# A first stage's order written anew: local attention and a PReLU feed-forward on one Trainium2 core

## The chip, the cores and the metric

The kernel runs on one core of one Trainium2 chip. The metric is the device time of one execution in microseconds (us), the median of several runs. Lower is better. The reference runs in fp32, and the kernel keeps fp32 accuracy by splitting operands into a high and a low fp32r part.

## The reference

Attention is local: each sequence of 576 positions is cut into chunks of 64, and a chunk attends to itself alone. The result, 4608 tokens of 512 numbers, goes through two dense layers with a PReLU between them.

```python
scores = scale * np.matmul(q_c, k_c.transpose(0, 1, 2, 4, 3))     # 8 x 8 x 9 chunks of 64 x 64
scores = scores - np.max(scores, axis=-1, keepdims=True)
attn = np.exp(scores)
attn = attn / (np.sum(attn, axis=-1, keepdims=True) + 1e-09)
out = np.matmul(attn, v_c)
x = np.ascontiguousarray(out.transpose(0, 2, 1, 3)).reshape(B * S, H * D)   # 4608 x 512
h = x @ w_in                                                      # 512 -> 2048
g = np.maximum(h, 0.0) + alpha * np.minimum(h, 0.0)
return (g @ w_out).astype(np.float32)                             # 2048 -> 512
```

## The kernel before

**Tiles.** Tokens come in sub-blocks of 128 (two chunks, all eight heads); four sub-blocks make a block of 512 tokens, nine blocks in all. The first three blocks use plain matmuls, the other six go in pairs with fewer products; that later part isn't touched. The weights of both layers come as 16 chunks each (`wi0` to `wi15` of w_in, `wo0` to `wo15` of w_out). Each is loaded as raw 64-bit words and turned into a high and a low part by seven steps on ScalarE (ACT) and VectorE (DVE) (`piece`, L180).

**The first stage** prepares the eight sub-blocks of blocks 0 and 1 and the first nine chunks of each side, and starts the dense layers. Its order is written out by hand in `START` (L28): a list of tokens that a loop (L931) turns into instructions one after the other, so each engine runs its share in just that order. After the list a scheduler places the rest. The tokens are:

- `q`, `k`, `v` with a number: a load of that sub-block's operand (sub-blocks 0 and 1 one by one, then two at a time). `wi3`, `wo3`: the load of a raw chunk.
- `W5`: five filler matmuls 128x128 of zeros on TensorE (PE), whose result nobody reads (L898).
- `S3`: the scores of sub-block 3 on PE, 16 matmuls 64x64 (L261). `m3`: their maxima on DVE (L298). `z3`, `e3`, `a3`, `r3`, `n3`: the rest of the softmax. In the usual way `z` scales the maxima, `e` is eight exponentials on ACT, one per head, each with its own bias and with a summing read-out (L313), `a` adds 1e-9 on GpSimd (POOL). For the sub-blocks in `SUBTRACTED`, `z` subtracts the maxima on DVE (L302), `e` is one exponential over all heads (L304), and `a` sums on DVE (L307). `n` multiplies by the reciprocals.
- `T3`: four transposes of the probabilities on PE (L349); `p3`: ACT copies them out (L356). `V3`: times the values on PE, 16 matmuls 64x64 (L367); `x3`, `l3`: high part by ACT (L373), low part by DVE (L375).
- `h02`: first layer of block 0, chunk 2, 12 matmuls 128x512 on PE (L422); `R`, `G`, `gh`, `gl`: the PReLU and the split (L407, L410, L436, L439). `o02`: second layer, 12 matmuls (L458). `K`: a result tile is stored (L492, L495).
- `wi3b`, `k`, `h`, `u`, `v`, `i`, `j`: the seven steps of chunk `wi3` (L194 to L209); `b` and `i` run on ACT, the others on DVE. A chunk named in `ALONE` has all steps on DVE.

`BANKS` says which pair of PSUM banks each S, T and V takes (`banks_of`, L243): 0, 1 and 2 are the pairs `ps_a`, `ps_oa`, `ps_ob`. Before, a transpose takes a whole pair and uses one bank of it. The fillers and the first layer rotate through the two buffers of `ps_h`. `HALVES` names the scratch tile of each chunk's split.

Of the kernel before, what the change touches and what calls it, by code (L numbers as in the profile page):

```python
# [10 lines left out]
F32 = mybir.dt.float32  # L11
# [8 lines left out]
def bits(pattern):  # L20
# [5 lines left out]


START = """  # L28
W8 q0 k0 k1 q1 q2 S0 W1 k2 m0 S1 W5 wi1 z0 m1 e0 wi0 z1 a0 e1 r0 S2 k4 n0 S3 m2 q4 wi1b z2 T0 W6 m3
e2 a1 z3 wi1k v0 wi0b r1 wi1h n1 wi2 p0 wi0k T1 a2 e3 wi0h r2 S4 W3 v2 wi0u n2 m4 q6 p1 V0 a3 z4  # L30
wi0v e4 T2 W4 k6 r3 wi0i wi1u wi0j wo4 wi1v x0 V1 n3 p2 wo0 l0 x1 V2 wi2b a4 l1 T3 x2 wo1 wi2k S5 p3
l2 wi1i V3 m5 v6 S6 r4 x3 z5 n4 e5 wi4 l3 h00 m6 v4 wi2h z6 wi1j e6 wi2u S7 wi3 a5 wi2v h01 m7 wo2
r5 R00 z7 n5 wo0b G00 wi5 wi2i T5 e7 wo0k wi2j h02 wi7 a6 wo0h r6 wo0u wo5 n6 p5 wo0v gh00 T6 wo1b
a7 T4 wo3 gl00 wo0i V5 r7 wo1k p6 wo0j x5 V6 n7 p4 l5 x6 T7 wo1h V4 l6 p7 wo1u x4 o00 R01 wo1v wo2b
G01 wo1i l4 gh01 wo1j R02 V7 gl01 o01 x7 wo2k G02 wi4b wi3b wo2h wo2u gh02 l7 h10 wo2v gl02 wo2i
wi3k wo2j wi4k wo4b o02 wi3h wi4h R10 wo4k wi4u K0 wi3u K1 G10 h11 wi4v gh10 wi3v wi4i gl10 K2 wi3i
wo4h wi4j K3 o10 wo4u wo5b wi3j R11 wo4v wi5b G11 wo4i wo6 h12 wo5k gh11 wo4j wi6 gl11 wo3b wo5h
wo3k wo5u wo8 o11 R12 wo3h wo5v wi8 G12 wo5i wo3u gh12 wo7 h13 wo5j gl12 wi7b wo3v wi5k wo3i wi7k
wi5h o12 R13 wo3j wi5u G13 wi5v gh13 h14 wi7h wi5i gl13 wi6b wi5j wi6k wi7u wi6h o13 R14 wi7v G14
wi7i wi6u gh14 wo6b wi6v h15 gl14 wi6i wo6k wi6j wi7j wo7b wo6h o14 wo7k R15 wo6u G15 wo6v gh15 wo7h  # L40
wi8b gl15 h16 wo6i wo7u wo7v wo6j wo7i wi8k o15 wo7j R16 wo8b G16 wi8h gh16 wi8u gl16 h17 wi8v wo8k
wi8i wi8j wo8h o16 R17 G17 wo8u gh17 wo8v gl17 wo8i wo8j
"""

ALONE = ('wi0',)
SUBTRACTED = (0,)
HALVES = {
    "wi1": "ta", "wi0": "tb", "wi2": "tc", "wo0": "tb", "wo1": "ta", "wo2": "tc", "wi4": "tb", "wi3": "ta",
    "wo4": "tc", "wo5": "tb", "wi5": "ta", "wo3": "tc", "wi7": "tb", "wi6": "tc", "wo6": "ta", "wo7": "tc",
    "wi8": "tb", "wo8": "ta",  # L50
}
BANKS = {
    "S0": 1, "S1": 2, "S2": 0, "S3": 1, "T0": 2, "T1": 0, "S4": 2, "V0": 1, "T2": 0, "V1": 2, "V2": 0, "T3": 1,
    "S5": 2, "V3": 1, "S6": 0, "S7": 1, "T5": 2, "T6": 1, "T4": 2, "V5": 0, "V6": 1, "T7": 2, "V4": 0, "V7": 0,
}
LISTED = 18

# [2 lines left out]
def tile_local_attention_prelu_ffn(  # L60
# [13 lines left out]
    P = 128  # L74
# [9 lines left out]
    TB = 512  # L84
# [147 lines left out]
    def attn_load(s, parts="qkv"):  # L232
# [61 lines left out]
    def early_softmax(s, sc3):  # L294
# [214 lines left out]
    n0, n1 = TURNS  # L509
# [369 lines left out]
    def start(token):  # L879
# [201 lines left out]
```

## Time and profile before

| what | value |
|---|---|
| median of three runs | 771.2 us (770.76 to 772.01) |
| span of the profiled execution | 770.2 us; its own time isn't listed apart, the median run lies 1.0 us above this span |
| PE busy | 760.4 us, 99% |
| DVE, ACT, POOL busy | 646.7, 447.3, 184.8 us |
| HBM traffic | 135.27 MB read, 42.99 MB written |

The span runs from the first to the last instruction. A busy PE says only that matmuls stand in its record: fillers count too, and so do slow matmuls. The timeline shows instructions with their start and length; rows of equal instructions are merged, and a bracket tells the idle time before them and who ended it. One 128x128 filler matmul shows as two records, one matmul 128x512 as one.

### The profile page before, as it was taken

What the parts mean: (1) busy time and instruction counts of PE and PEld (TensorE: products, weight loads), DVE (VectorE), ACT (ScalarE), POOL (GpSimd) and SP (SyncE); (2) the same over time, 40 slices, a digit from 0 to 9 for tenths busy, and PEclk for the clock granted to TensorE, in tenths of its full rate; (3) what the DMA queues carried; (4) which work ended last, traced back from release to release, by engine and by line L of the source; (5) the groups of instructions that cost most, each with busy time, mean ns of one, the idle gap of its engine ahead of it and who ended that gap; (6) DMA issues with size and microseconds to landing.
All of it is one profiled execution on the core that took longest, in us unless ns stands there. A gap on an engine that the chain in (4) does not pass through costs nothing.

```text
span 770.2 us, 15415 instructions
## 1 busy us (share of the span) xinstructions
PE 760.4 (99%) x5558; PEld 639.8 (83%) x5558; DVE 646.7 (84%) x1140; ACT 447.3 (58%) x1221; POOL 184.8 (24%) x304
## 2 busy tenths in 40 slices
PE   7999999999999999999999999999999999999998
PEld 7788887888888888888888888888888888888886
DVE  6999988989899886877899898777898977679784
ACT  6975555576666665666657456664574544354643
POOL 1153322343254331111121121111221121122110
PEclk9999999999999999999999999999999999999999
DMA  9859496468798775878765678875656765555573
GB/s 349 337 196 386 176 324 216 163 229 226 234 238 274 240 258 200 304 275 277 263 234 197 233 250 288 269 239 206 207 193 223 260 228 193 204 205 192 198 258 144
DMA packets 69322, 184.52 MB, mean 240 GB/s; under 512 B 10992, under 2 KB 18176, under 8 KB 69120
## 3 DMA queue, kind: packets, MB, share of 16 engines
q0 software_dynamic: 34336, 119.56, 45.9%
q1 hardware_dynamic: 34480, 63.20, 24.2%
q8 instruction: 44, 0.72, 0.4%
q10 hardware_dynamic: 432, 0.79, 0.3%
q14 instruction: 30, 0.25, 0.1%
HBM read 135.27 MB, written 42.99 MB: 231 GB/s over the span
## 4 chain that ended last, share of the span: by engine, by line
PE 92%; ACT 4%; DVE 2%; DMA 2%; issue 0%; ACTq 0%; SPq 0%
PE ps_o L722 20%; PE ps_o L850 19%; PE ps_h L422 14%; PE ps_h L722 10%; PE ps_h L850 10%; PE ps_oa L458 8%; PE ps_ob L458 7%; PE ps_a L388 2%; PE ps_a L272 2%; ACT wi L313 1%; ACT wo L313 1%; DMA raw<-w_in 1%; DMA raw<-w_out 1%; PE ps_h L898 1%; ACT wi L207 0%
## 5 line engine op out<-in xcount | busy, mean ns | idle before, releaser
L422 PE MATMUL ps_h<-xh,wi 128*128 128x512 f32 x384 | 101.7, 385 | 0.7 <-DVE g L410 0.5
L422 PEld LDWEIGHTS ps_h<-xh,wi 128*128 128x128 f32 x384 | 70.7, 187 | 13.8 <-DVE g L410 0.9
L722 PE MATMUL ps_o<-wi,raw 128*128 128x512 f32 x336 | 79.1, 382 | 0.0
L722 PEld LDWEIGHTS ps_o<-wi,raw 128*128 128x128 f32 x336 | 62.5, 187 | 11.2
L678 ACT CAST gh<-wo 128x512 fp32r<-128x512 f32 x66 | 41.0, 620 | 47.4 <-PE ps_o L850 31.8
L287 ACT ACTIVATE pr<-ps_a,mx 128x64 f32<-128x64 f32 x224 | 67.2, 325 | 0.8
L458 PE MATMUL ps_oa<-wo,gh 128*128 128x512 f32 x192 | 58.5, 385 | 0.1
L458 PE MATMUL ps_ob<-wo,gh 128*128 128x512 f32 x192 | 57.7, 380 | 0.0
L422 PE MATMUL ps_h<-xl,wi 128*128 128x512 f32 x192 | 50.6, 381 | 0.0
L679 DVE TENSOR_TENSOR gl<-wo,gh 128x512 fp32r<-128x512 f32 x63 | 43.2, 686 | 7.5 <-ACT gh L678 7.1
L287 ACT ACTIVATION_READ_ACCUMULATOR pr<-ps_a,mx 128x1 f32 x224 | 48.6, 217 | 0.0
L659 POOL DMA_DIRECT2D raw<-wi_a x42 | 22.3, 531 | 102.1 <-PE ps_o L722 54.5
L659 POOL DMA_DIRECT2D raw<-wo_a x42 | 22.2, 529 | 90.8 <-PE ps_o L850 51.2
L407 ACT ACTIVATE wo<-gh 128x512 f32<-128x512 f32 x24 | 15.2, 632 | 48.5 <-DVE gh L752 48.5
L678 ACT CAST ta<-wo 128x512 fp32r<-128x512 f32 x42 | 26.1, 621 | 26.4 <-PE ps_o L850 15.2
L422 PEld LDWEIGHTS ps_h<-xl,wi 128*128 128x128 f32 x192 | 35.8, 187 | 6.7 <-DVE xl L375 0.2
L458 PEld LDWEIGHTS ps_ob<-wo,gh 128*128 128x128 f32 x192 | 35.9, 187 | 6.4
L458 PEld LDWEIGHTS ps_oa<-wo,gh 128*128 128x128 f32 x192 | 35.3, 187 | 7.0 <-ACT gh L436 0.5
L722 PE MATMUL ps_o<-wi,wo 128*128 128x512 f32 x168 | 40.4, 383 | 0.0
L722 PE MATMUL ps_o<-wi,wi 128*128 128x512 f32 x168 | 40.4, 383 | 0.0
L722 PE MATMUL ps_h<-wi,raw 128*128 128x512 f32 x168 | 40.4, 382 | 0.0
L407 ACT ACTIVATE g<-ps_h 128x512 f32<-128x512 f32 x48 | 29.5, 614 | 17.5 <-PE ps_h L422 17.5
(296 smaller groups left out, 2036.2 us busy)
## 6 DMA issues: line engine op xcount, KB each, us to landing
raw<-wi_a POOLq DMA_DIRECT2D x42, 512.0 KB, 4.4
raw<-wo_a POOLq DMA_DIRECT2D x42, 512.0 KB, 3.5
wi<-wi_a POOLq DMA_DIRECT2D x21, 512.0 KB, 3.7
wo<-wi_a POOLq DMA_DIRECT2D x21, 512.0 KB, 4.3
wi<-wo_a POOLq DMA_DIRECT2D x21, 512.0 KB, 3.5
wo<-wo_a POOLq DMA_DIRECT2D x21, 512.0 KB, 3.6
k_sb<-kT SPq DMA_DIRECT2D x28, 256.0 KB, 4.7
q_sb<-qT SPq DMA_DIRECT2D x28, 256.0 KB, 4.1
```

Of the source, the lines that this page charges most:

```text
L272: pe(nc.tensor.matmul(att[0][c * C:(c + 1) * C, par, (NP + hp) * C:(NP + hp + 1) * C], lhsT=q_sb[rows, 2 * hp + c], rhs=kb[rows, 2 * hp + ...
L287: last = nc.scalar.activation(pr[:, g], sc3[:, g // NP, g % NP], AF.Exp, bias=mx[:, g], scale=SCALE, accum_out=sm[:, g])
L313: last = nc.scalar.activation(pr[:, g], sc3[:, g % 2, g // 2], AF.Exp, bias=mx[:, g], scale=SCALE, accum_out=sm[:, g])
L388: pe(nc.tensor.matmul(att[0][par * C:(par + 1) * C, c, hp * C:(hp + 1) * C], lhsT=v_sb[rows, h * C:(h + 1) * C], rhs=p[rows, :, par * NP + ...
L407: nc.scalar.activation(g, h, AF.Relu, scale=-1.0)
L422: pe(nc.tensor.matmul(woven(hps), lhsT=wi[f][:, l, k * P:(k + 1) * P], rhs=woven(xx[:, k]), start=(i == 0 and k == 0), stop=(i == 2 and k ...
L458: pe(nc.tensor.matmul(woven(o), lhsT=a[:, ts], rhs=woven(wo[f][:, l]), start=(f == first and i == 0), stop=(f == last and i == 2),))
L659: streamed[0] = nc.gpsimd.dma_start(out=f32(t), in_=units[side][n])
L678: hi = nc.scalar.copy(t_hi, t)
L679: return hi, nc.vector.tensor_tensor(t_lo, t, f32(t_hi), op=ALU.subtract)
L722: pe(nc.tensor.matmul(woven(ps), lhsT=w[:, l, k * P:(k + 1) * P], rhs=woven(xx[:, xl]), start=first and at == 0, stop=at == n - 1, skip_gr ...
L850: pe(nc.tensor.matmul(woven(ps[m]), lhsT=w[:, l, m * P:(m + 1) * P], rhs=woven(xx), start=i in (1, 5, 2) and j == 0 and n == 0, stop=j == ...
```

## The change

The list `START` is written anew, with the three tables that go with it. `SUBTRACTED` goes from sub-block 0 to sub-blocks 3 and 5. `BANKS` now counts single banks: 0 to 5 are the six banks of the three pairs, 6 and 7 mean a buffer of `ps_h`, which is the first layer's. A transpose takes one bank alone; S and V take the pair. The pairs are now made once and kept, where each token took a new tile of the pool before. `REMAINDERS` isn't used. The functions behind the tokens are the same.

```diff
 START = """
-W8 q0 k0 k1 q1 q2 S0 W1 k2 m0 S1 W5 wi1 z0 m1 e0 wi0 z1 a0 e1 r0 S2 k4 n0 S3 m2 q4 wi1b z2 T0 W6 m3
-e2 a1 z3 wi1k v0 wi0b r1 wi1h n1 wi2 p0 wi0k T1 a2 e3 wi0h r2 S4 W3 v2 wi0u n2 m4 q6 p1 V0 a3 z4
-wi0v e4 T2 W4 k6 r3 wi0i wi1u wi0j wo4 wi1v x0 V1 n3 p2 wo0 l0 x1 V2 wi2b a4 l1 T3 x2 wo1 wi2k S5 p3
...
+q0 k0 wi0 k1 W16 S0 q1 m0 W6 S1 q2 wi0b z0 wi0k k2 wi0h wi0u W12 S3 e0
+m1 wi1 a0 q4 z1 e1 wi0v r0 wi0i wi1b n0 S2 m3 m2 k4 T0 a1 v0 z3 p0
+r1 z2 e3 n1 e2 wi2 W14 S4 wi1k a3 wi0j m4 T1 r3 S5 v2 a2 p1 z4 e4
+n3 r2 m5 W4 V1 n2 T3 x1 a4 p3 wi1h k6 W3 T2 V0 z5 p2 wi1u W1 V3
+r4 q6 l1 x0 e5 V2 n4 x3 T4 l0 wo0 S6 x2 wi1v p4 l3 m6 wi2b l2 z6
+W3 S7 v4 h00 m7 wo0b wi1i wi1j z7 wo2 V4 e6 wi2k a5 a6 wi2h wo1 r5 wo0k n5
...
-SUBTRACTED = (0,)
+SUBTRACTED = (3, 5,)
+REMAINDERS = ()
...
 BANKS = {
-    "S0": 1, "S1": 2, "S2": 0, "S3": 1, "T0": 2, "T1": 0, "S4": 2, "V0": 1, "T2": 0, "V1": 2, "V2": 0, "T3": 1,
-    "S5": 2, "V3": 1, "S6": 0, "S7": 1, "T5": 2, "T6": 1, "T4": 2, "V5": 0, "V6": 1, "T7": 2, "V4": 0, "V7": 0,
+    "S0": 2, "S1": 0, "S2": 2, "S3": 4, "S4": 4, "S5": 0, "S6": 4, "S7": 0, "T0": 6, "T1": 7, "T2": 7, "T3": 6, "T4": 6, "T5": 0, "T6": 4, "T7": 5, "V0": 4, "V1": 2, "V2": 2, "V3": 0, "V4": 2, "V5": 0, "V6": 2, "V7": 4,
 }
...
+    pairs = {}
+
     def banks_of(token):
-        pool, name = ((ps_a, "ps_a"), (ps_o, "ps_oa"), (ps_o, "ps_ob"))[BANKS[token]]
-        return pool.tile([P, 2, TB], F32, name=name)
+        pair, bank = divmod(BANKS[token], 2)
+        if pair == 3:
+            return ps_h.tile([P, TB], F32, name="ps_h")
+        if pair not in pairs:
+            pool, name = ((ps_a, "ps_a"), (ps_o, "ps_oa"), (ps_o, "ps_ob"))[pair]
+            pairs[pair] = pool.tile([P, 2, TB], F32, name=name)
+        return pairs[pair][:, bank] if token[0] == "T" else pairs[pair]
...
-        tp = banks_of(f"T{s}")[:, 0]
+        tp = banks_of(f"T{s}")
```

Three places show what the new list does. The first is the beginning of PE's program; rows on `ident` are transposes, 64x64 rows on `wo_96`/`wo_98` or `wi_97`/`wi_99` are scores, rows on `wo_109` are fillers. Before:

```order
L898 MATMUL ps_h<-wo_109 128x128 x8
L261 MATMUL ps_oa<-wo_96,wo_98 64x64 x16
L898 MATMUL ps_h<-wo_109 128x128
L261 MATMUL ps_ob<-wo_96,wo_98 64x64 x16
L898 MATMUL ps_h<-wo_109 128x128 x5
L261 MATMUL ps_a<-wi_97,wi_99 64x64 x16
L261 MATMUL ps_oa<-wi_97,wi_99 64x64 x16
L349 MATMUL ps_ob<-ident,wo_100 128x128 x4
L898 MATMUL ps_h<-wo_109 128x128 x6
L349 MATMUL ps_a<-ident,wo_100 128x128 x4
L261 MATMUL ps_ob<-wo_96,wo_98 64x64 x16
L898 MATMUL ps_h<-wo_109 128x128 x3
```

With the change:

```order
L906 MATMUL ps_h<-wo_109 128x128 x16
L269 MATMUL ps_oa<-wo_96,wo_98 64x64 x16
L906 MATMUL ps_h<-wo_109 128x128 x6
L269 MATMUL ps_a<-wo_96,wo_98 64x64 x16
L906 MATMUL ps_h<-wo_109 128x128 x12
L269 MATMUL ps_ob<-wi_97,wi_99 64x64 x16
L269 MATMUL ps_oa<-wi_97,wi_99 64x64 x16
L357 MATMUL ps_h<-ident,wo_100 128x128 x4
L906 MATMUL ps_h<-wo_109 128x128 x14
L269 MATMUL ps_ob<-wo_96,wo_98 64x64 x16
L357 MATMUL ps_h<-ident,wo_100 128x128 x4
L269 MATMUL ps_a<-wo_96,wo_98 64x64 x16
```

The first scores stand behind 16 fillers instead of 8, and the fillers between the groups are 6, 12 and 14 instead of 1, 5 and 6; the transposes write to `ps_h`.

The second place is ACT's program at the softmaxes of the first sub-blocks; rows `x8` are the eight exponentials of one sub-block, rows without it on `wo_100` or `wi_101` the single one. Before:

```order
L304 ACTIVATE wo_100<-wo_100 128x512
L313 ACTIVATE wo_100,sm<-ps_ob,mx 128x64 x8
L194 ACTIVATE ta<-raw 128x512
L313 ACTIVATE wi_101,sm<-ps_a,mx 128x64 x8
L356 COPY wo_102<-ps_ob 128x512
L313 ACTIVATE wi_101,sm<-ps_oa,mx 128x64 x8
```

With the change:

```order
L321 ACTIVATE wo_100,sm<-ps_oa,mx 128x64 x8
L321 ACTIVATE wo_100,sm<-ps_a,mx 128x64 x8
L195 ACTIVATE tb<-raw 128x512
L364 COPY wo_102<-ps_h 128x512
L312 ACTIVATE wi_101<-wi_101 128x512
L321 ACTIVATE wi_101,sm<-ps_oa,mx 128x64 x8
```

Sub-blocks 0 and 1 both have eight exponentials now, and sub-block 3 has a single one, ahead of sub-block 2's eight.

The third place is SP's queue just behind the list, where the scheduler places loads and stores: `raw<-w_in` is a chunk's load, `partial` are the four stores of block 1's first partial result. Before:

```order
L178 DMA raw<-w_out 128x512
L236 DMA q_sb<-qT 128x512
L495 DMA partial_0_1446<-q_sb 128x512
L495 DMA partial_1_1450<-v_sb 128x512
L495 DMA partial_2_1454<-v_sb 128x512
L495 DMA partial_3_1458<-pr 128x512
L178 DMA raw<-w_in 128x512
```

With the change:

```order
L179 DMA raw<-w_out 128x512
L237 DMA q_sb<-qT 128x512
L179 DMA raw<-w_in 128x512
L503 DMA partial_0_1458<-q_sb 128x512
L503 DMA partial_1_1462<-v_sb 128x512
L503 DMA partial_2_1466<-v_sb 128x512
L503 DMA partial_3_1470<-pr 128x512
```

The load of raw chunk `wi12` stands ahead of the four stores instead of behind them.

## Rows read from the trace of the kernel before

**Rows 1.** The page, busy time of each engine over the span.
```profile
PE 760.4 (99%) x5558; PEld 639.8 (83%) x5558; DVE 646.7 (84%) x1140; ACT 447.3 (58%) x1221; POOL 184.8 (24%) x304
```

**Rows 2.** Busy time by stretch: PE, PEld, DVE, ACT, POOL, PEclk, DMA, GB/s.
```profile
8.00:25.00 17.00, 13.10 (x342) 11.14 (x340) 16.20 (x39) 16.16 (x83) 1.66 (x4) 1.00 1.02 403
...
41.00:86.00 45.00, 45.00 (x228) 38.24 (x220) 43.93 (x83) 28.76 (x48) 19.62 (x26) 1.00 0.79 286
86.00:128.00 42.00, 41.50 (x189) 34.72 (x188) 37.28 (x70) 22.47 (x40) 11.12 (x15) 1.00 0.74 257
```

**Rows 3.** Who PE waited for: us in total, times, longest.
```profile
PE ps_ob L349 <- ACT wo L313: 1.1, 1, 1.1
...
PE ps_a L349 <- DVE tb L196: 0.9, 1, 0.9
...
PE ps_h L422 <- DVE g L410: 0.5, 1, 0.5
```

**Rows 4.** Timeline of PE, first stage: start, length, instruction, idle before.
```profile
1.06 3.78 PE L898 MATMUL ps_h<-wo 128*128 128x128 f32 x16 [1.06 <-DVE table L147]
4.77 1.13 PE L261 MATMUL ps_oa<-wo,wo 64*64 64x64 f32 x32
5.83 0.79 PE L898 MATMUL ps_h<-wo 128*128 128x128 f32 x2
6.56 0.97 PE L261 MATMUL ps_ob<-wo,wo 64*64 64x64 f32 x32
7.46 1.38 PE L898 MATMUL ps_h<-wo 128*128 128x128 f32 x10
8.95 0.69 PE L261 MATMUL ps_a<-wi,wi 64*64 64x64 f32 x32
9.43 0.68 PE L261 MATMUL ps_oa<-wi,wi 64*64 64x64 f32 x32
11.18 0.63 PE L349 MATMUL ps_ob<-ident,wo 128*128 128x128 f32 x4 [1.07 <-ACT wo L313]
11.64 1.50 PE L898 MATMUL ps_h<-wo 128*128 128x128 f32 x12
...
18.02 1.06 PE L898 MATMUL ps_h<-wo 128*128 128x128 f32 x8
...
24.14 1.15 PE L422 MATMUL ps_h<-xh,wi 128*128 128x512 f32 x4 [0.24 <-ACT xh L373]
...
27.10 0.69 PE L261 MATMUL ps_oa<-wi,wi 64*64 64x64 f32 x32
27.73 1.15 PE L422 MATMUL ps_h<-xh,wi 128*128 128x512 f32 x4
...
41.28 0.72 PE L458 MATMUL ps_oa<-wo,gh 128*128 128x512 f32 x2
```

**Rows 5.** Chain of waits, first stage: one first-layer step, 12 matmuls, start and length.
```profile
44.22 2.64 PE ps_h L422 x12
```

**Rows 6.** Timeline of ACT: single exponential; first of a sub-block's eight; the copy behind them.
```profile
7.42 0.63 ACT L304 ACTIVATE wo<-wo 128x512 f32<-128x512 f32 x1 [4.75 <-DVE wo L302]
...
14.26 0.43 ACT L313 ACTIVATE wi<-ps_oa,mx 128x64 f32<-128x64 f32 x1
...
16.58 0.75 ACT L356 COPY wo<-ps_a 128x512 f32<-128x512 f32 x1
```

**Rows 7.** Timeline of DVE: sub-block 0's maxima, subtraction and sum.
```profile
5.97 0.69 DVE L298 TENSOR_REDUCE mx<-ps_oa 128x8 f32<-128x512 f32 x1 [4.96 <-PE ps_oa L261]
6.70 0.69 DVE L302 TENSOR_TENSOR wo<-ps_oa,mx 128x512 f32<-128x512 f32 x1
...
8.41 0.68 DVE L307 TENSOR_REDUCE sm<-wo 128x8 f32<-128x512 f32 x1
```

**Rows 8.** Timeline of SP, ACT and PE behind the list.
```profile
100.45 0.70 SPq L495 DMA_DIRECT2D partial<-pr  x1
101.27 1.13 SPq L178 DMA_DIRECT2D raw<-w_in  x1
...
108.41 0.71 ACT L194 ACTIVATE tc<-raw 128x512 f32<-128x512 f32 x1 [2.12 <-DMA raw<-w_in]
...
126.74 1.15 PE L422 MATMUL ps_h<-xh,wi 128*128 128x512 f32 x4 [0.50 <-DVE g L410]
```

More of the change, by code (lines that the diff above doesn't have):

```diff
@@ L28 @@
 START = """
-W8 q0 k0 k1 q1 q2 S0 W1 k2 m0 S1 W5 wi1 z0 m1 e0 wi0 z1 a0 e1 r0 S2 k4 n0 S3 m2 q4 wi1b z2 T0 W6 m3
-e2 a1 z3 wi1k v0 wi0b r1 wi1h n1 wi2 p0 wi0k T1 a2 e3 wi0h r2 S4 W3 v2 wi0u n2 m4 q6 p1 V0 a3 z4
-wi0v e4 T2 W4 k6 r3 wi0i wi1u wi0j wo4 wi1v x0 V1 n3 p2 wo0 l0 x1 V2 wi2b a4 l1 T3 x2 wo1 wi2k S5 p3
-l2 wi1i V3 m5 v6 S6 r4 x3 z5 n4 e5 wi4 l3 h00 m6 v4 wi2h z6 wi1j e6 wi2u S7 wi3 a5 wi2v h01 m7 wo2
-r5 R00 z7 n5 wo0b G00 wi5 wi2i T5 e7 wo0k wi2j h02 wi7 a6 wo0h r6 wo0u wo5 n6 p5 wo0v gh00 T6 wo1b
@@ L34 @@
[L34 to L39, printed above, removed]
@@ L40 @@
-wi7i wi6u gh14 wo6b wi6v h15 gl14 wi6i wo6k wi6j wi7j wo7b wo6h o14 wo7k R15 wo6u G15 wo6v gh15 wo7h
-wi8b gl15 h16 wo6i wo7u wo7v wo6j wo7i wi8k o15 wo7j R16 wo8b G16 wi8h gh16 wi8u gl16 h17 wi8v wo8k
-wi8i wi8j wo8h o16 R17 G17 wo8u gh17 wo8v gl17 wo8i wo8j
+q0 k0 wi0 k1 W16 S0 q1 m0 W6 S1 q2 wi0b z0 wi0k k2 wi0h wi0u W12 S3 e0
+m1 wi1 a0 q4 z1 e1 wi0v r0 wi0i wi1b n0 S2 m3 m2 k4 T0 a1 v0 z3 p0
+r1 z2 e3 n1 e2 wi2 W14 S4 wi1k a3 wi0j m4 T1 r3 S5 v2 a2 p1 z4 e4
+n3 r2 m5 W4 V1 n2 T3 x1 a4 p3 wi1h k6 W3 T2 V0 z5 p2 wi1u W1 V3
@@ new lines @@
+r4 q6 l1 x0 e5 V2 n4 x3 T4 l0 wo0 S6 x2 wi1v p4 l3 m6 wi2b l2 z6
+W3 S7 v4 h00 m7 wo0b wi1i wi1j z7 wo2 V4 e6 wi2k a5 a6 wi2h wo1 r5 wo0k n5
+e7 v6 x4 h01 a7 r6 wo0h R00 wi2u wi4 R01 n6 r7 n7 T5 wi5 l4 T6 wi2v wi3
+p5 p6 wo4 G00 T7 wo0u p7 V5 wi2i wo3 V6 wo1b V7 x6 wi7 G01 wi2j x7 l6 x5
+gh00 wo6 h02 l7 gh01 l5 wo0v gl00 wo2b wo0i R02 wo0j wo1k wi4b h10 G02 wo1h wo2k o00 wo1u
+wo2h wo1v gl01 wo1i gh02 wo2u wo1j h11 wi3b o01 wo2v gl02 wo2i R11 wi4k wi3k wo2j wi4h R10 wo3b
+wi8 G10 G11 wi4u gh10 o02 K1 gl10 h12 wo7 wi4v wo3k gh11 wo3h wi4i wi4j K0 K3 wi3h wo3u
@@ new lines @@
+wi6 K2 wi5b wi3u gl11 R12 o10 wo3v wi5k wo3i wi3v G12 wi3i wi5h gh12 wi3j wo3j gl12 o11 wo4b
+wi5u wo5 wi6b h13 wo4k h14 R13 wo4h wi5v wi5i wo4u wi6k wo4v wi6h G13 wo4i gh13 o12 wi6u wo4j
+wi5j wi6v h15 wo5b wo5k wi6i gl13 R14 wo6b o13 wo5h wi6j G14 gh14 wo6k wo5u wo8 wi7b gl14 wi7k
+wo6h wi7h wo5v wo6u R15 wi7u wo6v h16 wo5i wi7v G15 wo6i wi7i wo5j o14 wo6j gh15 wi8b wi7j gl15
+wo7b wi8k R16 wo8b G16 wo8k wi8h wo7k gh16 wo8h h17 wi8u gl16 o15 wo8u wo7h wi8v wo8v wo7u R17
+wo8i G17 wo7v wi8i wo8j gh17 wo7i wi8j wo7j gl17 o16
@@ L43 @@
 """
 ALONE = ('wi0',)
-SUBTRACTED = (0,)
+SUBTRACTED = (3, 5,)
+REMAINDERS = ()
 HALVES = {
-    "wi1": "ta", "wi0": "tb", "wi2": "tc", "wo0": "tb", "wo1": "ta", "wo2": "tc", "wi4": "tb", "wi3": "ta",
-    "wo4": "tc", "wo5": "tb", "wi5": "ta", "wo3": "tc", "wi7": "tb", "wi6": "tc", "wo6": "ta", "wo7": "tc",
-    "wi8": "tb", "wo8": "ta",
+    "wi0": "ta", "wi1": "tb", "wi2": "tc", "wi3": "tb", "wi4": "ta", "wi5": "ta", "wi6": "tc", "wi7": "tc", "wi8": "tb", "wo0": "ta", "wo1": "tb", "wo2": "tc", "wo3": "tc", "wo4": "tb", "wo5": "tb", "wo6": "ta", "wo7": "ta", "wo8": "tc",
```

## The prediction

> **What bounds the kernel now.** I read the page first: PE is busy 99% of the span [rows 1]. That share can't be taken at its word, because fillers are in it, so the next views are the stretches and the timeline. From 41 to 86 us PE is busy 45.00 of 45.00 us [rows 2], and one layer step of 12 matmuls takes 2.64 us there [rows 5], which is 0.22 us per matmul without a gap. Behind that the only wait of PE that counts is one of 0.50 us at 126.74 [rows 3, 8]. So once the dense layers run, PE's own work sets the end, and that work is the same in both kernels: the scores, transposes, values, first and second layers are moved, none is added or dropped. A microsecond that PE spends on anything else in the first stage stays in the total, unless the one later wait swallows some of it. The question is how much of the first stage is not work.
>
> Before, take PE from its first filler at 1.06 to 41.28 [rows 4], where the steady part starts: 40.2 us. The work in it is 16 groups of scores or values at 0.62 (27.10 to 27.73), 8 groups of transposes at 0.46 (11.18 to 11.64) and four layer steps at 2.64 [rows 4, 5]: 9.9 + 3.7 + 10.6 = 24.2. The other **16.0 us** are 27 fillers, the waits (the longest in [rows 3]) and scores that ran slowly at first.
>
> **What the change does to it, part by part.**
>
> *Fillers.* 27 become 59: 16, 6, 12, 14, 4, 3, 1 and 3. PE runs its program in order, so each is paid, unless PE would have waited there anyway. Two prices stand in the rows [rows 4]. At the start eight take 1.06 to 4.77, 0.46 each. Later six take 1.50 and four 1.06, so one more costs 0.22; a group behind scores or values costs some 0.1 to 0.2 more to start (five take 1.38, where 5 x 0.22 is 1.10). [...] The granted clock reads 1.00 in every stretch of [rows 2], so the start shows in the lengths alone.
>
> The leading sixteen: the first eight end at 4.77 as before. The next eight cost between 8 x 0.22 = 1.8 (full clock at once) and 8 x 0.46 = 3.7 (half clock to the end). If the clock rises near 7.2, as the rows of before have it, five run slowly and three fast: 3.0. PE does other work in these microseconds than before, so the rise can come sooner; I take 2.6, inside the bounds. S0 then starts at 7.4 (6.6 to 8.5) instead of 4.77, and 1.06 to 7.4 is 6.3 us that are not work.
>
> The other 43: 43 x 0.22 = 9.5, and seven starts at some 0.15 make 10.6.
>
> *Waits that are left on PE.* With PE this full, the others mostly get ahead of it. One wait I can see: T2's buffer of `ps_h` is the one that T3 used, two rotations before, so T2 waits for the copy p3. On ACT that copy stands behind sub-block 4's eight exponentials, 2.32 us (14.26 to 16.58) [rows 6], and x1. S4 comes near 18; maxima and scaling take 0.9 [rows 7], the exponentials 2.3 and x1 and p3 half a microsecond each, while PE needs some 4.5 us from S4 to T2 (four groups, seven fillers). T2 waits about 0.7 (0 to 1.0). Small starts between layer steps and 64-wide groups add 0.5.
>
> Not work after the change: 6.3 + 10.6 + 0.7 + 0.5 = 18.1. Scores or values that follow each other directly take 0.48 rather than 0.62 (8.95 to 9.43) [rows 4]; the new list has four such pairs and the old one one, which gives back 0.4. The balance is 18.1 - 0.4 - 16.0 = **+1.7 us**, between +0.9 and +2.8 by the bounds of the first group alone.
>
> *Subtraction on DVE.* Sub-block 0 goes back to eight exponentials, 3 and 5 leave them: ACT saves 2.32 - 0.5 = 1.8 us net; DVE pays one more subtraction and sum, 0.69 + 0.68 [rows 7], and some 0.1. Taken at nothing: both engines are hidden behind PE's fillers. The check: sub-block 0's maxima come at 8.2 instead of 5.97. From there to the last low part of block 0 DVE has 24 wide instructions at 0.6, six at 0.34 and ten small ones at 0.1: 17.5, and a microsecond of waits makes 27. ACT has four times 2.32, two single exponentials, five copies, four high parts and one chunk step, 15 us from 9.2 with a microsecond or two of waits: 26. PE reaches h00 at 7.4 + 7.2 (scores and values) + 2.3 (transposes) + 10.6 + 0.7 = 28.2, instead of 24.14 [rows 4]. Both arrive first. If the cover of a microsecond or two is gone, PE waits by what is missing.
>
> *Banks.* Transposes in `ps_h` free the pairs for scores and values. That takes away waits such as the 1.1 us of T0 for the exponentials that read its bank [rows 3]; in the new list fillers stand there, so nothing is gained by it. The pairs aren't the limit with PE this full, so the kept pairs cost nothing either.
>
> *Loads.* `wi0` (512 KB) is put ahead of `k1` on SP: at 403 GB/s [rows 2] it costs 1.3 us. S1 ran at 6.56 [rows 4], so `k1` was there by then and is there by 7.9 now; S1 stands at about 9.5. Nothing. `q4` waits in SP's queue for S1 to let go of its buffer; what is issued ahead of it, some 3 MB, keeps the queues busy until about 10.
>
> *Behind the list.* From the end of the list to about 130 us the scheduler mixes the steps of the layers differently; from there on PE's two programs are the same. The load of `wi12` was issued at 101.27 behind the four stores, and ACT waited 2.12 us for it at 108.41 [rows 8]; that delay reaches DVE's queue, and PE's wait of 0.50 at 126.74 is for a DVE result held up there. Now the load stands ahead of the stores. I think the wait goes: **-0.5**. The bounds are -0.5 and, if DVE, which is 2 us later at first, stays behind, some +0.7.
>
> The sum is 1.7 - 0.5 = **+1.2**. It is made against the profiled execution, span 770.2; the median run is 1.0 above that, which nothing here changes. So 771.2 + 1.2 = **772.4 us**, 0.16%, less than the 0.2% (1.5 us) that a measurement of this kernel can tell from no change.
>
> **The rivals.** *The clock rises late, and the wait stays.* If the half clock holds through all 16 fillers as it held to 7.2 before, S0 comes at 7.8 to 8.5, 0.4 to 1.1 later than I take, and if DVE's later start keeps the wait at 126 us, 0.5 isn't got back: +2.1 to +2.8, about 773.6, slower. It decides from S0 at 7.7 on. For it: the slow scores at 6.56. Against: only one execution tells where the clock rose. Chance 0.36.
>
> *The clock rises early.* If 16 full-width fillers in a row bring the full clock right behind the eighth, S0 starts at 6.6, 0.8 before my value, and the time is 771.6. In the rows PE was busy from 1.06 and the clock still rose only between 6.6 and 7.5, behind scores that fill a part of the array. [...] Chance 0.14, part of "no change".
>
> *ACT was the path.* ACT is busy 16.16 of 17 us from 8 to 25 [rows 2], and two of PE's longest waits are for its exponentials. If the eight exponentials set the pace and the fillers only fill what PE would wait for, the 1.8 us saved on ACT come off: 769.4, faster. Against it: the fillers stand in program order ahead of the scores that feed ACT, and S0 alone is 2 us later. Chance 0.04.
>
> **How the numbers follow.** My forecast has 0.46, the early clock 0.14: together 0.60 for within 0.2%. The late clock with the wait kept has 0.36 for slower, ACT as the path 0.04 for faster. The range leaves out the last case and the far end of the slow one: from 770.8 (early clock, wait gone, 0.8 for the terms read off small gaps) to 774.0 (late clock, wait kept, 0.4 for a wait more).
>
> **What would show it.** In the profile after: 118 filler records (54 before), S0 near 7.4, h00 near 28.2, one wait of PE for ACT's copy near 23, hardly any other before 41 us, ACT with more idle time up to 28 us than before, no wait of PE near 127 us. Wrong would be: h00 before 26 us, or PE waiting several microseconds in the first stage on top of its fillers, or a wait of PE after 90 us that is longer than the 0.50.

## The result, and the profile after

The changed kernel takes **776.56 us** (median of four, 775.97 to 777.2), the kernel before 771.13 beside it: a ratio of **1.0065** (95% interval 1.0051 to 1.0079), slower by 5.4 us. The forecast was 772.4 and its range ended at 774.0.

The profiled execution of the changed kernel has a span of 774.8 us and took 776.66. The time of an execution is some 1.8 us above its span in nearly all runs here. So the profiled execution of before, span 770.2, was the slowest of its three (772.0), 0.8 above their median: the two traces differ by 4.6 us, not by 5.4.

The page's busy times of the changed kernel; [rows 1] answers to it. The added records are fillers.

```profile
PE 766.8 (99%) x5622; PEld 647.1 (84%) x5622; DVE 647.4 (84%) x1142; ACT 445.8 (58%) x1206; POOL 184.6 (24%) x303
```

The stretches of [rows 2] after the change, columns as there, and one of 1.5 us:

```profile
8.00:25.00 17.00, 16.94 (x366) 15.40 (x367) 15.55 (x36) 14.40 (x73) 0.96 (x4) 1.00 0.96 355
41.00:86.00 45.00, 45.00 (x206) 38.23 (x205) 44.18 (x84) 29.15 (x51) 18.09 (x24) 1.00 0.75 261
86.00:128.00 42.00, 42.00 (x192) 35.72 (x191) 38.79 (x73) 24.03 (x43) 12.84 (x16) 1.00 0.76 263
...
10.50:12.00 1.50, 1.50 (x16) 1.50 (x16) 1.47 (x4) 1.50 (x12) 0.15 (x1) 1.00 0.59 76
```

PE is full from 8 to 25 us (13.10 before), VectorE and ScalarE do less in the same time (15.55 and 14.40; before 16.20 and 16.16). From 10.5 to 12 the loads fall to 76 GB/s, because `q4` waited on SyncE for S1.

Who PE waited for behind 5 us, the whole list of it, where [rows 3] stood:

```profile
PE ps_ob L357 <- DVE tc L203: 1.3, 1, 1.3
PE ps_ob L269 <- issue: 0.9, 1, 0.9
PE ps_o L858 <- DMA raw<-wo_a: 0.8, 1, 0.8
PE ps_a L357 <- ACT wi L321: 0.2, 1, 0.2
```

And PE's timeline, answering to [rows 4]. L906 are fillers, L269 scores, L357 transposes, L430 first layer, L466 second layer.

```profile
1.06 6.33 PE L906 MATMUL ps_h<-wo 128*128 128x128 f32 x32 [1.06 <-DVE table L148]
7.32 0.69 PE L269 MATMUL ps_oa<-wo,wo 64*64 64x64 f32 x32
...
26.03 0.56 PE L269 MATMUL ps_ob<-wi,wi 64*64 64x64 f32 x20
27.50 0.45 PE L269 MATMUL ps_ob<-wi,wi 64*64 64x64 f32 x12 [0.91 <-issue]
...
29.37 1.15 PE L430 MATMUL ps_h<-xh,wi 128*128 128x512 f32 x4
...
35.99 0.66 PE L357 MATMUL ps_a<-ident,wo 128*128 128x128 f32 x4 [0.20 <-ACT wi L321]
36.48 0.60 PE L357 MATMUL ps_ob<-ident,wi 128*128 128x128 f32 x4
38.41 0.66 PE L357 MATMUL ps_ob<-ident,wi 128*128 128x128 f32 x4 [1.33 <-DVE tc L203]
...
394.36 0.50 PE L858 MATMUL ps_o<-gh,raw 128*128 128x512 f32 x1 [0.80 <-DMA raw<-wo_a]
```

S0 starts at 7.32 as forecast. Then three things stand there that the forecast did not have: the scores of S6 stop in their middle for 0.91 us with nothing to wait for ("issue"); T7 (at 38.41) waits 1.33; T5 (at 35.99) waits 0.20.

How far the changed kernel is behind is read by counting the matmul records that are still to come. From 55 to 121 us of before it is 4.5 us behind, where the forecast had 1.7. Then before's wait of 0.50 at 126.74 [rows 8] is gone, and with the slow starts around it that gives back 1.0: of the last 4500 records, which come in the same order in both kernels, the first begins at 133.1 us before and at 136.6 after. The wait at 394.36 brings the last microsecond.

VectorE's first maximum, whose row before is in [rows 7], moved from 5.97 to 8.08:

```profile
8.08 0.69 DVE L306 TENSOR_REDUCE mx<-ps_oa 128x8 f32<-128x512 f32 x1 [7.07 <-PE ps_oa L269]
```

### The profile page after: what moved, and what is told of

Its sections match the earlier page's. It is cut to its first block, busy times and chain, and to the rows that moved or that the text cites. A ratio compares the mean times of both kernels' runs of the same rounds, so it can differ in the third digit from the quotient of the medians.

```text
span 774.8 us, 15558 instructions
## 1 busy us (share of the span) xinstructions
PE 766.8 (99%) x5622; PEld 647.1 (84%) x5622; DVE 647.4 (84%) x1142; ACT 445.8 (58%) x1206; POOL 184.6 (24%) x303
## 4 chain that ended last, share of the span: by engine, by line
PE 82%; issue 11%; POOL 2%; DMA 2%; DVE 1%; ACT 1%; SPq 1%; POOLq 0%; DVEq 0%
PE ps_o L858 19%; PE ps_h L430 14%; PE ps_o L730 13%; PE ps_h L858 10%; PE ps_oa L466 7%; PE ps_ob L466 7%; PE ps_h L730 6%; PE ps_h L906 2%; PE ps_a L396 2%; PE ps_a L280 1%; DMA raw<-wo_a 1%; POOL raw L667 1%; SPq L346 1%; POOL wi L667 0%; POOL wo L667 0%
## 5 line engine op out<-in xcount | busy, mean ns | idle before, releaser
L430 PE MATMUL ps_h<-xh,wi 128*128 128x512 f32 x384 | 101.5, 385 | 0.0
L430 PEld LDWEIGHTS ps_h<-xh,wi 128*128 128x128 f32 x384 | 70.8, 187 | 12.8
L466 PE MATMUL ps_oa<-wo,gh 128*128 128x512 f32 x192 | 58.2, 383 | 0.0
L466 PE MATMUL ps_ob<-wo,gh 128*128 128x512 f32 x192 | 57.9, 380 | 0.0
L430 PE MATMUL ps_h<-xl,wi 128*128 128x512 f32 x192 | 50.1, 381 | 0.0
L430 PEld LDWEIGHTS ps_h<-xl,wi 128*128 128x128 f32 x192 | 35.9, 187 | 6.5
L466 PEld LDWEIGHTS ps_ob<-wo,gh 128*128 128x128 f32 x192 | 35.9, 187 | 6.3
L466 PEld LDWEIGHTS ps_oa<-wo,gh 128*128 128x128 f32 x192 | 35.6, 187 | 6.3
```

The source lines that it names most:

```text
L430: pe(nc.tensor.matmul(woven(hps), lhsT=wi[f][:, l, k * P:(k + 1) * P], rhs=woven(xx[:, k]), start=(i == 0 and k == 0), stop=(i == 2 and k ...
L466: pe(nc.tensor.matmul(woven(o), lhsT=a[:, ts], rhs=woven(wo[f][:, l]), start=(f == first and i == 0), stop=(f == last and i == 2),))
```

## The experiments

All changes are against the changed kernel unless a diff says otherwise. "Step" is the start of the second layer's first step, 45.97 us in the changed kernel. Ratios are to runs of before on the same chip; the changed kernel's is 1.0065.

**Are the fillers paid?** First the leading ones, then the later ones:

```diff
-q0 k0 wi0 k1 W16 S0 q1 m0 W6 S1 ...
+q0 k0 wi0 k1 W8 S0 q1 m0 W6 S1 ...
```

> The changed list with 8 leading fillers instead of 16, nothing else. Theory F (PE's program alone is the path, every filler in it is paid): S0 at 4.8 us instead of 7.32, h00 2.5 us earlier (26.9 instead of 29.37), and the time 2.5 us less, 774.1. Theory D (from the first scores on VectorE and ScalarE have no slack and pace the later part; what counts is when S0 comes): the same 2.5 us or nearly, because VectorE's first maximum comes 2.3 us earlier; but PE then waits more at T5 and T7 only if it gets ahead of them. Rival C (the scores would run at half clock instead of the fillers): S0 and S1 take about 0.4 us more each, and 1.5 to 1.8 us are left of the gain: 774.8 to 775.1.

Measured: 777.06 us, 1.0066 (1.0048 to 1.0084): nothing gained. S0 stands at 4.77, 2.5 us earlier; behind its slow scores PE is 1.9 us ahead from S1 to S6, and in the fillers ahead of S7 it stops:

```profile
24.80 0.71 PE L906 MATMUL ps_h<-wo 128*128 128x128 f32 x4
27.71 0.38 PE L906 MATMUL ps_h<-wo 128*128 128x128 f32 x2 [2.21 <-issue]
```

h00 comes at 28.65, 0.7 earlier instead of 2.5, and waits of 0.5 and 0.2 near 136 and 137 us take that back. None of the three theories had this.

The second run takes out W6, W12, W14, W4, both W3 and W1, and keeps W16.

> The changed list with the 16 leading fillers and none of the 43 later ones. Theory F: 43 x 0.22 and the starts, about 10 us less on PE; even if a good part turns into waits, 4 us or more are gained: 772 or less. Theory D: VectorE works without a pause worth the name from 8.08 to 26.6 us, so the fillers stand where PE would wait for it; only the 1.35 us that VectorE waited for S6 at 27.99 and a few tenths before can be got back: 1.3 to 2 us less, 774.5 to 775.3, with 8 us or more of new waits of PE between 8 and 29 us. Rival C: with PE idle in between the scores, values and layers run at half clock for some microseconds: the granted clock or the length of a layer step shows it (more than 2.64 us), and the time is the same or more than 776.6.

Measured: 775.38 us, 1.0045 (1.0032 to 1.0059), step at 44.65. Theory D holds and theory F falls: 43 fillers less, some 10 us of PE's time, give 1.3 us in the list. In their place stand waits, for loads (1.8 and 1.3), for VectorE (1.0, 0.5) and for ScalarE (0.9, 0.7). VectorE has no pause over 0.25 us from 8.31 to 32.86. Rival C is there in part: the granted clock is 0.73 on average from 8 to 20 us (1.00 in the changed kernel), and four transposes take 1.09 us at 13.71 where they take 0.66 at 24.52, so some of PE's freed time goes into slower matmuls. The fillers stand where PE would wait or run slowly.

**T7's wait.** T6 and T7 take the two banks of one pair, `ps_ob`.

```diff
-    ... "T6": 4, "T7": 5, ...
+    ... "T6": 4, "T7": 3, ...
```

> The changed list with T7 in the second bank of ps_oa instead of ps_ob's, whose other bank T6 fills. Theory B (T7 waits 1.33 us for ScalarE's copy of T6, which reads the other bank of the same pair and ends at 38.37): T7 waits for the last reader of ps_oa, l4, that ends at 37.78, and starts at 37.8 instead of 38.41; 0.6 us less on PE, 776.0. Rival R (T7 waits for the VectorE instruction that the waits name, which ends at 38.38, or for something behind it): T7 still starts at 38.4, no change.

Measured: 775.47 us, 1.0048 (1.0035 to 1.0060). T7 now waits 0.8 for `xl` (l4), as theory B has it. The step is 1.22 earlier, but 0.8 of that is S0, which stood at 6.52 in this execution; what is left is the bank's 0.4. So the wait was for the copy out of the other bank, and the name in the list of waits (VectorE, L203) was a coincidence of ends: 38.38 there, 38.37 for the copy.

**The subtractions.**

```diff
-SUBTRACTED = (3, 5,)
+SUBTRACTED = ()
```

> The changed list with no sub-block subtracting its maxima on VectorE: 3 and 5 take eight exponentials like the others (ScalarE some 1.8 us more each, VectorE 1.4 us less each). Theory F: the work off PE is hidden, no change, within 0.3 us. Theory D with VectorE as the pace: the chain r5, n5, e7 comes 1.3 to 2.7 us earlier, T7's wait of 1.33 and T5's of 0.2 vanish, 1 to 1.5 us less, 775.1 to 775.6. Theory D with ScalarE as the pace (it is busy 7.81 of 8 us from 20 to 28): the exponentials of 5 push x0, p4 and the rest back, PE waits 1 to 2.5 us more, 777.6 to 779.

Measured: 776.44 us, 1.0061 (1.0048 to 1.0074), step at 45.96. In this list sub-block 5's exponentials then read their pair behind V3, which overwrites it, so the output is not the reference's; every instruction still runs. No difference, but the halt (1.0) and T7's wait (1.3) are still there and may hide one.

**The halt.** Is it the loads, or the number of instructions?

> The changed list with 8 leading fillers and none of the 43 later ones. Theory D (VectorE paces the first stage; in the run without the later fillers it was busy without a pause of more than 0.25 us from 8.31 to 32.86): S0 comes 2.5 us earlier, VectorE starts 2.2 earlier, and the list ends 1.4 to 2.2 us earlier than there (k4's load, that S4 waited for at 16.06, takes the rest): 773.2 to 774.0. Theory I (PE's instructions come too late whatever the list does before, as the halt of 2.21 us at 27.7 in the run with 8 leading fillers suggests): a halt marked issue of 1.5 us or more between 24 and 28 us, and the time as without the later fillers, 775.0 to 775.6. Theory F (every filler is paid): some 12 us less PE work than the changed list has, 765 to 768.

Measured: 774.93 us, 1.0044 (1.0031 to 1.0057), step at 45.46. A halt of 2.7 us before 25.07, inside V2: theory I. The start that came 2.5 us earlier is lost again; the granted clock fell around the halt too (0.77 on average from 20 to 28 us, 0.88 from 28 to 41), and how much of the loss that is was not separated. The traced execution is the slowest of seven, which go from 772.72 to 775.80.

Then fillers of the same length with fewer instructions:

```diff
-            for _ in range(s):
+            for _ in range(s // 4):
+                nc.tensor.matmul(hps, lhsT=plain, rhs=plain[:, :1].broadcast_to([P, TB]), start=True, stop=True)
+            for _ in range(s % 4):
                 nc.tensor.matmul(hps[:, :P], lhsT=plain, rhs=plain, start=True, stop=True)
```

> The changed list whose fillers are 512 columns wide, one for every four (59 become 23, of the same length together); the rest as it is. Theory I (the halt of 0.91 us in the middle of S6 is PE out of instructions: it stopped at the same place of the program, matmul record 472, in the changed kernel and with 8 leading fillers, and the fetch marked instruction ended 1.3 to 1.4 us before it went on): 72 matmul records fewer ahead of S6 put that place into the layer steps, where a matmul takes 0.22 us: no halt in S6 or S7, VectorE's pause of 1.35 at 27.99 shrinks to 0.4 or less, and the list ends 0.9 to 1.1 us earlier: 775.5. Rival M (the halt is a thing of the time, DMA queues at full load until 26 us, not of the number of instructions): a halt of 0.7 us or more stays near 27, 776.4.

Measured: 776.16 us, 1.0063 (1.0047 to 1.0078); its profiled execution took 775.30. S6 and S7 run through (L908 are the narrow fillers that are left):

```profile
25.08 0.69 PE L269 MATMUL ps_ob<-wi,wi 64*64 64x64 f32 x32
25.70 0.94 PE L908 MATMUL ps_h<-wo 128*128 128x128 f32 x6
26.57 0.69 PE L269 MATMUL ps_a<-wi,wi 64*64 64x64 f32 x32
27.19 1.16 PE L430 MATMUL ps_h<-xh,wi 128*128 128x512 f32 x4
...
38.52 0.46 PE L375 MATMUL ps_ob<-wi,wi 64*64 64x64 f32 x16 [0.31 <-issue]
```

h00 is 2.2 us earlier than in the changed kernel; 1.0 of it is S0 (6.33 here), most of the rest the halt. A small halt is left, later. So the halt is a matter of how many instructions stand ahead of that point. The median moved by less than the list did (1.6); run to run this kernel goes from 775.3 to 777.6.

That PE was out of instructions is read from three things. Counting matmul records from the start, every halt over 0.15 us in these runs stands behind record 345, 472 or 598, 126 or 127 apart, whatever the list had there: 472 in the changed kernel, in the run with 8 leading fillers, and in those with T7's bank, without subtractions and with the third buffer; 345 in the run just above with a halt of 2.7, and 598 with wide fillers and in the run without the later ones. The DMA view has one instruction packet of 16 KB ahead of each; from 25 to 26 us in the changed kernel it reads

```profile
q1 hardware_dynamic: 115, 0.41, 101.2%
q8 instruction: 1, 0.02, 5.9%
```

and PE goes on 1.3 to 1.5 us behind that packet's end in every one of them (ended 26.11, on at 27.50; with 8 leading fillers 26.46 and 27.71). Queue q8 carries 45 such packets in the changed kernel, for PE's 11,244 matmul and weight-load records 250 each; the step of 126 or 127 matmul records, each with its weight load, is 252 or 254.

Read so, PE went through a packet no faster than the next one came. By the lengths in the timelines (0.62 us for a 64x64 group of 32 records, 0.22 for a layer's matmul) I estimate that 126 records last four such groups, some 2.4 us, or some 28 us of layer steps. While the load queues are full (DMA at 1.0 up to some 35 us) the packets came 6 to 10 us apart; in the changed kernel they begin at 10.38, 18.35, 25.16, 31.15 and 41.23. The new list has S7, T4 and 32 fillers more ahead of h00; before reached record 472 inside h01, at 29.16, and halts nowhere. That the full load queues are what holds the packets back was not tried by itself. The traces agree with it: behind record 345, with the DMA share at 1.0, the next packet begins 2.2 to 4.3 us after that record in all eighteen; behind record 598 it begins 0.3 to 0.6 us after it in the four traces where no transfer ran in between.

**Sub-block 7's exponentials.** They started at 33.45, 1.50 us behind the sixth's; their sums take the buffer that sub-block 5 had.

```diff
-            sm = small.tile([P, H, 1], F32, name="sm", bufs=2)
+            sm = small.tile([P, H, 1], F32, name="sm", bufs=3)
```

> The changed kernel with three buffers instead of two for the sums of the softmax, the list untouched. Theory N (sub-block 7's exponentials wait 1.50 us before 33.45, because their sums take the buffer that sub-block 5's normalisation reads until 33.34; what follows, T7 above all, comes late by that): they start at 31.95, right behind sub-block 6's; T5 no longer waits 0.20, and T7's 1.33 shrink to 0.5 to 0.8, because the copies p5 and p6 then wait for h01's end (35.9) behind R01: 0.7 to 1.0 us less, 775.6 to 775.9. Rival R (they wait for something else that ends at 33.4): no change, 776.6.

Measured: 775.82 us, 1.0059 (1.0043 to 1.0076), step at 44.55; 0.6 of the 1.4 is S0 at 6.72. T5 waits no longer, and T7's wait falls as theory N has it, now with the copy's name:

```profile
37.01 0.66 PE L357 MATMUL ps_ob<-ident,wi 128*128 128x128 f32 x4 [0.78 <-ACT wi L364]
```

**The later start, in the list of before.**

```diff
-W8 q0 k0 k1 q1 q2 S0 ...
+W16 q0 k0 k1 q1 q2 S0 ...
```

> The kernel before with 16 leading fillers instead of 8, its list and all else untouched. Theory D (what counts is when S0 comes; VectorE is busy from its first maximum on and has 1.3 us of pauses from 8 to 41): S0 at 7.3 instead of 4.77, VectorE's first maximum 2.1 us later, the list 1.0 to 2.2 us later: 772.3 to 773.4 where before has 771.2 to 771.6. Theory F (all of it is paid): 2.5 us later, 773.8. Rival L (the loads pace the first stage, queues are busy until 25 us): no change, 771.4.

Measured: 773.44 us, 1.0029 (1.0019 to 1.0038), S0 at 7.13. Eight more leading fillers in before's list cost 2.2 us by themselves.

**All of it undone, step by step.** Wide fillers with 8 leading; then the third buffer too; then T7's bank too.

> The changed list with wide fillers (one of 512 columns for every four) and 8 leading ones (2 wide) instead of 16. Theory I+D (with 8 narrow leading fillers the 2.5 us were given back because PE ran out of instructions at 24.8; with 36 fewer fillers in its program it does not): S0 at 4.8, no halt above 0.4 us before 29, h00 1.5 us earlier than with wide fillers alone (27.19, where S0 stood at 6.33), the second layer's first step at 42.8 instead of 44.33: 774.0 to 774.7. Rival L (k4's load, that S4 waits for near 16, and the load queues pace the stage): S0 early, but a wait of PE or VectorE of 1 to 1.5 us near 16, and the second layer's first step at 43.8 or later: 775.5 or more.

> The same and three buffers for the sums of the softmax. Theory I+D+N: sub-block 7's exponentials start right behind sub-block 6's, T7's wait falls from 1.33 to 0.8, T5 does not wait; the second layer's first step at 42.2: 773.4 to 774.1. Rival B (VectorE, busy without a pause from 6 us, has become the bound behind the list): the list ends earlier as expected, but waits of PE for VectorE's results of 0.5 to 1 us stand between 100 and 165 us, and the time is that without the third buffer.

> The same and T7 in ps_oa's second bank, so that it waits for no copy of ScalarE. Theory B+N: T7 waits for l4 only, which follows sub-block 7's normalisation on VectorE: its wait falls from 0.8 to 0.4 or less; the second layer's first step at 41.8, 4.2 us earlier than in the changed kernel, which is all that its list took more than that of before: 772.2 to 773.5, what is left above before's 771.2 being waits behind the list. Rival B (VectorE bounds behind the list): no better than 773.4.

Measured: 774.72, 773.85 and 773.02 us; 1.0032 (1.0015 to 1.0049), 1.0033 (1.0023 to 1.0042) and 1.0023 (1.0013 to 1.0032); steps at 43.50, 42.95 and 42.06. The first lies between its two theories, the others near the first of theirs; by the ratios the first two can't be told apart. With 8 leading fillers the gain is now kept, because PE no longer runs out for 2.2 us behind 25.5 (halts of 0.26 us and less are left at record 345). In the last no wait of PE over 0.2 us is left from 5 us on, and the record that began at 136.6 begins at 132.7.

**The rest.** Is it the later fillers, VectorE, or the clock?

> The kernel with wide fillers, 8 leading ones, the third sums buffer and T7 moved; of its 43 later fillers 12 are taken out (6 to 4, 12 to 8, 14 to 12, 3 to 1, 1 to 0 and the last 3 kept; counted in narrow ones). Theory F' (with the waits gone PE's program is the path again: it ran there without a wait from 5 to 42 us): 11 x 0.22 = 2.4 us less, the second layer's first step at 39.7, 770.6. Theory D (VectorE takes over: it paused 0.63, 0.26, 0.33 and 0.69 us for PE before 26): 1.0 to 1.5 us less, 771.5 to 772.0, and waits of PE of a microsecond or more come back. Rival S (the rest over before's 771.2 is not in the list at all): no change, 773.0.

> The same with none of the 43 later fillers. Theory D: VectorE is without a pause, 771.3 to 772.0, no better than with 31 of them, PE waits 6 us or more between 8 and 27. Rival C (idle time of PE lets the clock fall, as the scatter from 772.7 to 775.8 and the granted clock of 0.988 to 1.0 in the run with 8 leading and no later fillers suggest): granted clock under 0.997 in most executions, layer steps or transposes at double length between 8 and 30 us, 772.5 to 775. Theory F': 9.5 us less, 763.5.

> As the run without the 43 later fillers, and no sub-block subtracts on VectorE (3 and 5 take eight exponentials). Theory D with VectorE as the pace: 2.7 us less work on VectorE before its last normalisation, 1 to 2 us less than with the subtractions. Theory D with ScalarE as the pace: 3.6 us more of exponentials on ScalarE, 1 to 3 us more. If neither engine paces there: within 0.5 us.

Measured: 772.57, 772.52 and 774.56 us; 1.0022 (1.0012 to 1.0032), 1.0015 (1.0006 to 1.0024) and 1.0043 (1.0030 to 1.0055). Taking out 12 or all 43 gives half a microsecond, less than theory D gave, though the list ends 0.7 to 0.8 earlier; by the ratios (1.0023, then 1.0022 and 1.0015) this can't be told from rival S, no change. Theory F' is out. Without them in the second run the stretch from 8 to 20 us, with PE idle between its groups, had a mean granted clock of 0.59, and four transposes take 1.11 us at 12.17 where they take 0.66 at 22.22, as rival C has it (columns as in [rows 2]):

```profile
8.00:20.00 12.00, 9.30 (x216) 7.50 (x212) 11.58 (x28) 11.71 (x68) 0.85 (x4) 0.59 1.01 393
20.00:28.00 8.00, 6.43 (x176) 5.23 (x175) 6.89 (x16) 7.03 (x22) 0.66 (x1) 1.00 1.03 411
```

With 31 of them the clock is 1.00 there. But the lower clock cost next to nothing: VectorE and ScalarE are busy 11.6 and 11.7 of the 12 us, as with the 31 fillers. The third run again has sub-block 5 behind V3, and S4 waits 3.1 us for sub-block 3's exponentials, now eight, which read its pair: it says that this order needs the subtraction, not what a subtraction costs.

In the first two the list ends earlier than before's (132.0 and 131.9 against 133.1 us, the latter in an execution 0.8 above its median), and the time is still above it. Behind the list stand new waits, as this one for transposed probabilities in the first:

```profile
190.80 0.63 PE L396 MATMUL ps_a<-pT,v_sb 64*64 64x64 f32 x27 [0.53 <-DMA pT<-t]
```

In ten of the traces with the new list the stretch around this place is 0.3 to 1.2 us longer than in before's; in those of before's list never. From the first of the last 4500 records to the end, the three traces of before's list take 637.1 to 637.2 us, the fifteen of the new one 637.3 to 639.8, all but one of them at least 637.6. The attention of later sub-blocks is placed at fixed layer steps, the visits. The last two runs move the visit at this place by one step, and put the new subtractions into before:

```diff
-    visits = [42, 46, 50, 54, 57, 60, 64, ...
+    visits = [42, 46, 50, 54, 57, 61, 64, ...
```

> The kernel with 31 of the later fillers (wide, 8 leading, third sums buffer, T7 moved), and the attention visit that stands before step 60 moved before step 61. Theory T (its list already ends 1.1 us ahead of before's, and the waits behind it eat that: 0.5 for transposed probabilities at 190 us, 0.3 around 140): the wait of 0.53 at 190.8 goes, 0.4 to 0.6 us less, 772.0 to 772.2. Rival V (VectorE and SyncE's queue are late there, whatever the visit's place): the wait turns up at the next visit, 772.6.

```diff
 (the kernel before)
-SUBTRACTED = (0,)
+SUBTRACTED = (3, 5)
```

> The kernel before, its own list, with the sub-blocks 3 and 5 subtracting their maxima on VectorE instead of 0: that part of the change alone. My prediction's term (hidden on both engines): 771.2, within 0.3 us. Theory D with VectorE as the pace of the first stage (11.51 of 12 us busy from 8 to 20, 12.54 of 13 from 28 to 41): 1.4 us more work on VectorE, 0.7 to 1.4 us more, 771.9 to 772.6. With ScalarE as the pace (11.45 of 12, 12.64 of 13): 1.8 us less work there, 0.5 to 1.5 us less, 769.7 to 770.7; but sub-block 0's exponentials, that everything starts with, become eight, 1.8 us longer on the way to T0.

Measured: 772.68 us, 1.0016 (1.0007 to 1.0024), and 773.76 us, 1.0029 (1.0018 to 1.0040). In the first nothing is gained; the wait at 190 is gone and 0.4 turns up at the next visit, as rival V has it, but in an execution whose list ended late, so this trace alone doesn't settle it. That execution, the slowest of eleven (774.43; the others from 772.0 on), shows one thing that makes these kernels scatter:

```profile
PE ps_oa L375 <- issue: 3.0, 1, 3.0
PE ps_a L269 <- DMA wo<-kT: 1.1, 1, 1.1
```

The same place, record 345, held the run with 12 fillers taken out for 1.1 us with the same program up to there; this one's list ends 3.05 later. In the second run, on before's list, the change of sub-blocks costs 2.4 us. PE's longest waits are two of before's, both longer: T0's for sub-block 1's exponentials, which stand behind sub-block 0's, now eight (1.7, before 1.1), and V1's for sub-block 4's (1.8, before 0.7):

```profile
PE ps_ob L367 <- ACT wo L313: 1.8, 1, 1.8
PE ps_ob L349 <- ACT wo L313: 1.7, 1, 1.7
```

The granted clock fell here too, to 0.86 from 8 to 20 us and 0.79 from 20 to 28 (1.00 in before's trace); how much of the 2.4 that is was not separated.

No version beats before: the best is within 0.06% to 0.24% above it.

## Why the prediction was wrong, step by step

*Fillers.* Their number and lengths came as forecast: 118 records, 6.3 us to S0, and 10.9 us from start to start for the seven later groups, where 10.6 were forecast. That the doubled price at the start is a half clock, on which the 2.6 us for the second eight rest, no run shows: the granted clock reads 1.00 from 0 to 8 us in both kernels. What the changed kernel showed in its place is a spacing of the filler records that falls from 0.21 to 0.11 us, and 2.7 us for the second eight. But of "each is paid, unless PE would have waited there anyway" the second half holds for most of the later ones: without the 43 the changed list gains 1.3 us and the mended one half a microsecond. They fill waits for VectorE, ScalarE and the loads, and the granted clock from 8 to 20 us is 1.00 with them, 0.73 and 0.59 without the 43. What costs in before's list is the leading group, 2.2 us, because everything else starts with S0; in the changed list the halt took its gain back.

*Waits.* This is the step that failed: "hardly any other [wait] before 41 us". The forecast wait of 0.7 at T2 did not come: T2 starts at 22.72, 0.4 before ScalarE's copy p3 (23.11) that it was to wait for. The halt, T7's and T5's waits did. The profile gives them 0.91, 1.33 and 0.20 of idle time; from start to start they cost more. S6 takes 1.85 us to the fillers behind it instead of 0.62, T6 1.93 to T7 instead of 0.46, the last four matmuls of h01 1.25 to T5 instead of 0.88: 3.1 together. 1.7 - 0.7 + 3.1, and 0.3 more for the fillers, make 4.4 of the 4.5 by which the list is later. The halt is PE without instructions, which the forecast has no term for; T7's wait is taken apart below.

*Banks,* "the kept pairs cost nothing either": they do. T7, a transposition into the second bank of a pair, waited for the copy out of the first; in another pair its wait was 0.8 instead of 1.33.

*Subtraction on DVE,* taken at nothing: the cover was judged at h00 alone, and there VectorE was early, as the forecast had it. The chain behind it was not followed: sub-block 5's normalisation, late in VectorE's new order, holds the buffer of sums that sub-block 7 needs; with a third buffer T5's wait goes and T7's falls from 1.33 to 0.78 (without the subtraction T7's wait was the same as with it). That the change of sub-blocks costs nothing by itself holds at most in the changed list; in before's it costs 2.4.

*Loads,* nothing: `q4` did open a hole of 1.5 us at 10.5, where "busy until about 10" was forecast. No wait of PE in the changed kernel shows it; when fillers go, PE waits for `k` loads.

*Behind the list,* -0.5: the wait at 126 us did go, and gave back 1.0. The sign of being wrong, "a wait of PE after 90 us that is longer than the 0.50", came true at 394 us (0.80), and other runs of the new list have theirs at 190. Why the new list has more of them is open; VectorE, at 44.2 of 45 us up to 86, has little to give, but this was not tried.

*The base.* "the median run is 1.0 above that, which nothing here changes" took the distance of time to span for a fixed 1.0. It is 1.8, so the profiled run of before was itself 0.8 slow, and a change read from that trace is too small by as much.

*The rivals.* The late clock gave a time nearer to the result, but not its mechanism: S0 came at 7.32, below the 7.7 from which it decides. In the changed kernel the spacing of the filler records falls from 0.21 to 0.11 us at 6.3 us, where the forecast had the rise near 7.2. The early rise is real, though: with 16 leading fillers S0 stood at 7.32, 7.55, 6.52, 7.25 and, with wide ones or the third buffer, 6.33 and 6.72, so in these traces the point differs from run to run. ScalarE as the path: not seen; the list without subtractions, with more work for ScalarE, ended at the same time, and before's list with less of it ran longer.

Of the 5.4 us, then, wide fillers with 8 leading, a third buffer and T7 elsewhere give back 3.5; 12 fillers less give 0.5 more, inside the scatter; 1.2 to 1.8 stay, read as waits behind the list and as halts that come and go. That last part was read from traces, not undone by a run.

## What to carry to other kernels

Before you price a filler or a moved group on a full engine, ask what that engine would have waited for there, and follow the chain of the next engine to its end, buffers that are handed on included, not only to the first meeting point. Count instructions as well as microseconds where small tiles run in a row beside full load queues: an engine can run out of program, as PE is read to have done here for 0.91 us at record 472. And set a trace's own execution against the median before a sum is made on it.

## What the runs showed of the hardware that was not expected

PE's program is read as coming in packets of 16 KB: queue q8 carried 45 in the changed kernel, for 5622 matmul records and as many weight loads. PE went on 1.3 to 1.5 us behind the packet's end, and halts of 0.16 to 3.03 us stood at the same three records in thirteen kernels, under "issue" in the list of waits. The same program to that point halted 1.1 us in one execution and 3.0 in another. Under the same 16 narrow fillers, busy from 1.06 us on, the spacing of their records fell from 0.21 to 0.11 us at 4.6 us in one execution and at 6.8 in another, and S0 stood between 6.52 and 7.55 in six traces. The profile's idle time understates what a halt costs: 0.91 us of it made S6 1.23 us longer.
